# A one-token attention and gated-MLP kernel: residual rows ahead of the gate, later block jumps, wo in two loads, another syncing engine, and one wait for both stores

## The chip, the cores and the metric

One core of a Trainium2 chip. The metric is the device time of one execution in microseconds (us); medians of several executions are given. The profile's own span, from the program's first instruction to the end of its last, is about 2 us shorter than the device time. A load has "landed" when the last of the 16 DMA engines that share it has reported to its semaphore. The "tail" is what follows the attention loop, and "the granted clock" is the share of its full clock at which TensorE was allowed to run.

## The reference, cut to what matters

One decoding step for a batch of 2: layer norm, attention of 32 heads over a cache of 8192 positions, then layer norm and a gated MLP (ReLU gate). Everything is bf16.

```python
h  = x + attention(layernorm(x), k_cache, v_cache, wq, wo)   # x: (2, 1, 512)
n  = layernorm(h)
gate, up = n @ W_gate, n @ W_up                              # (512, 1376) each
h2 = h + (relu(gate) * up) @ W_down                          # W_down: (1376, 512)
```

The two caches are 134 MB each and are read once; all weights together are 12.6 MB. So about 281 MB have to cross from HBM (281.06 MB read, by the page) for a few KB of input and output rows.

## The kernel before

Each engine has a list of operations with waits. The lists of TensorE, VectorE and ScalarE are printed in three blocks (all, last, rest): an engine runs the first part, jumps to "rest", and jumps back to "last" for the end; `s.cut(engine)` marks where "last" begins. The tail of the kernel, which is all that the change touches, looks like this:

```python
WO = ((0, 0, JG), (1, 0, JG // 2), (1, JG // 2, JG))      # wo in three loads (SyncE's queue)
# ... then gate, up0, up1 (three quarters and one quarter of W_up), and W_down as wda, wdb, wdc, wdd
# ... attention rows (TensorE), transpose, ar = copy of the rows (ScalarE), mean, hd = h - mean
s.op("pe", lambda: mlp_in(0, gate_ps, 0, KC), reads=["hd", "gate"], ...)
# variance (TensorE); r2, gt = relu(gate) * r2 (VectorE)
up_mostly = s.op("pe", lambda: mlp_in(1, up_ps, 0, KC - 1), reads=["hd", "up0"], ...)
s.wait("pe", [s.last["up1"]])
s.op("pe", lambda: mlp_in(1, up_ps, KC - 1, KC), reads=["hd", "up1"], ...)
s.cut("pe")
s.op("pe", lambda: y_rows(eye_of[:, 0:B], ar, first=True), reads=["eye", "om"], writes=["y"])  # residual
# gn (VectorE)
s.wait("dve", [up_mostly])
s.cut("dve")
# actr = gt * up, actn = gn * up (VectorE); columns_of_act, columns_of_rest (TensorE)
s.wait("act", [s.last["up1"]])
s.cut("act")
s.op("act", lambda: act.activation(out=act_t[:, 0:FA], in_=act_ps, func=ACT.Copy), reads=["sm"], ...)
# add_y over wda, wdb, wdc, wdd: 8 + 8 + 4 + 2 matmuls into y; VectorE and ScalarE copy half of y each
# two stores (SyncE and ScalarE); then
s.wait("pool", ends)                                      # both stores landed
s.lists["pool"].append(((), lambda: pool.sem_clear(range(min(sems), max(sems) + 1)), None))
```

The softmax here doesn't subtract the row's maximum and nothing guards it: scores larger than these inputs give would overflow.

## Time and profile before

| | before |
|---|---|
| device time, median of 3 | 658.21 us (658.06 to 658.22) |
| span of the profile | 656.2 us |
| VectorE busy | 612.7 us (93%) |
| data moved | 281.12 MB, 428 GB/s over the span |
| last weight packet moved | 652.60 us |
| last landing of W_down | 653.08 us |
| last store landed | 655.24 us |

The page's first part, a row of busy time, share of the span and instructions for each engine, and its line for the data queue (packets, MB, share of the time of 16 DMA engines):

```profile
PE 120.3 (18%) x1212; PEld 49.8 (8%) x1212; DVE 612.7 (93%) x172; ACT 63.2 (10%) x161; POOL 6.4 (1%) x27
q1 hardware_dynamic: 6596, 281.06, 99.3%
```

Two resources are nearly full. The 99.3% is the one to read as the bound: VectorE's 93% leaves it 43 us of idle time, while the 0.7% that the data queue lacks is less than what lies before its first packet (1.97 us) and behind its last weights.

### The profile page before, as it was taken

What the parts mean: (1) busy time and instruction counts of PE and PEld (TensorE: products, weight loads), DVE (VectorE), ACT (ScalarE), POOL (GpSimd) and SP (SyncE); (2) the same over time, 40 slices, a digit from 0 to 9 for tenths busy, and PEclk for the clock granted to TensorE, in tenths of its full rate; (3) what the DMA queues carried; (4) which work ended last, traced back from release to release, by engine and by line L of the source; (5) the groups of instructions that cost most, each with busy time, mean ns of one, the idle gap of its engine ahead of it and who ended that gap; (6) DMA issues with size and microseconds to landing.
All of it is one profiled execution on the core that took longest, in us unless ns stands there. A gap on an engine that the chain in (4) does not pass through costs nothing.

```text
span 656.2 us, 3121 instructions
## 1 busy us (share of the span) xinstructions
PE 120.3 (18%) x1212; PEld 49.8 (8%) x1212; DVE 612.7 (93%) x172; ACT 63.2 (10%) x161; POOL 6.4 (1%) x27
## 2 busy tenths in 40 slices
PE   2400302103030110302003030300303030031256
PEld 1100101001010000101001010100101010010012
DVE  0699999999999999999999999999999999999973
ACT  2501001010101001010100101010010101001021
POOL 3000000000000000000000000000000000000000
PEclk9855755657565565756556575555657556565756
DMA  9999999999999999989999999989999999999997
GB/s 380 451 443 411 423 447 447 423 407 447 447 447 391 439 447 447 443 387 447 447 447 415 415 447 447 443 387 447 447 447 427 403 447 447 443 403 432 425 420 311
DMA packets 6613, 281.12 MB, mean 428 GB/s; under 512 B 744, under 2 KB 848, under 8 KB 1360
## 3 DMA queue, kind: packets, MB, share of 16 engines
q1 hardware_dynamic: 6596, 281.06, 99.3%
q8 instruction: 2, 0.03, 0.0%
q14 instruction: 3, 0.02, 0.0%
q10 hardware_dynamic: 12, 0.01, 0.0%
HBM read 281.06 MB, written 0.00 MB: 428 GB/s over the span
## 4 chain that ended last, share of the span: by engine, by line
DVE 75%; DMA 24%; issue 0%; SPq 0%; PE 0%
DVE k L386 34%; DVE k L391 33%; DMA k<-in_A_k_cache_dram 21%; DVE sc L243 4%; DMA k<-in_B_W_down_dram 3%; DVE osb L471 2%; DVE om L466 1%; SPq L547 0%; DVE ou L243 0%; SPq L559 0%; DVE rep L478 0%; PE y L641 0%; DVE sc L721 0%; SPq L294 0%; SPq L805 0%
## 5 line engine op out<-in xcount | busy, mean ns | idle before, releaser
L386 DVE TENSOR_TENSOR k<-k,qrep 128x32768 bf16<-128x32768 bf16 (+3 forms) x18 | 275.8, 15322 | 6.2 <-DMA k<-in_A_k_cache_dram 6.1
L391 DVE TENSOR_TENSOR k<-k 128x8192 bf16<-128x8192 bf16 (+4 forms) x69 | 266.9, 3868 | 2.4
L417 PE MATMUL o<-v,pm 128*32 128x512 bf16 x1024 | 93.8, 544 | 478.8 <-PEq L432 478.8
L404 ACT ACTIVATE pm<-sc 32x256 bf16<-32x256 f32 (+2 forms) x68 | 48.0, 705 | 560.1 <-DVE sc L243 559.3
L417 PEld LDWEIGHTS o<-v,pm 128*32 128x32 bf16 x1024 | 38.5, 130 | 533.5 <-issue 527.7
L243 DVE TENSOR_REDUCE sc<-k 128x256 f32<-128x2048 bf16 (+2 forms) x17 | 36.6, 2151 | 0.1
L471 DVE TENSOR_REDUCE osb<-om 128x128 f32<-128x512 f32 x16 | 16.3, 1018 | 0.6
L404 ACT ACTIVATION_READ_ACCUMULATOR pm<-sc 32x1 f32 x68 | 15.7, 231 | 0.0
L466 DVE TENSOR_TENSOR om<-o,turn_of 128x512 f32<-128x512 f32 x16 | 10.9, 682 | 3.9 <-PE o L417 3.9
L350 PE MATMUL mm<-v,om 128*64 x32 | 9.5, 432 | 6.6 <-PEq L348 6.6
L243 DVE TENSOR_REDUCE pick<-ident 128x8 f32<-128x128 bf16 x1 | 0.4, 382 | 10.7 <-ACT qrep L367 10.7
L367 ACT ACTIVATE qrep<-mm 32x512 bf16<-32x512 f32 x16 | 9.4, 587 | 6.1 <-PE mm L350 5.2
L451 PE MATMUL rep<-osb,spread 128*32 128x128 f32 x32 | 2.6, 421 | 37.1 <-DVE osb L471 37.1
L538 POOL TENSOR_TENSOR zm<-zm,zx 128x1 f32<-128x1 f32 x1 | 0.2, 192 | 625.9 <-PE o L417 625.9
L320 DVE COPY xc<-st 128x8 f32<-128x8 f32 x1 | 0.2, 167 | 6.5 <-PE st L315 6.5
L350 PEld LDWEIGHTS mm<-v,om 128*64 128x64 bf16 x32 | 3.9, 121 | 11.8 <-issue 11.0
L607 DVE STREAM_TRANSPOSE osb<-mm 128x512 f32<-128x512 f32 x1 | 0.7, 716 | 3.8 <-PE mm L593 3.8
L593 PE MATMUL mm<-k 128*2 128x512 bf16 x32 | 3.8, 621 | 0.3 <-DMA k<-in_A_wo_dram 0.3
L451 PEld LDWEIGHTS rep<-osb,spread 128*32 128x32 f32 x32 | 0.8, 140 | 37.5 <-DVE osb L471 37.5
L446 PE MATMUL sm<-zm,same 128*128 128x16 f32 x8 | 1.8, 297 | 0.4 <-PEq L432 0.4
L721 DVE CAST sc<-y 2x256 bf16<-2x256 f32 x1 | 0.4, 413 | 1.5 <-PE y L641 1.5
L240 POOL MEMSET pm<- 128x2048 bf16 x1 | 1.8, 1805 | 0.1
(81 smaller groups left out, 34.9 us busy)
## 6 DMA issues: line engine op xcount, KB each, us to landing
v<-in_A_v_cache_dram SPq DMA_DIRECT2D x4, 4096.0 KB, 20.3
k<-in_A_k_cache_dram SPq DMA_DIRECT2D x2, 4096.0 KB, 26.3
v<-in_A_wq_dram SPq DMA_DIRECT2D x1, 4096.0 KB, 12.4
k<-in_A_wo_dram SPq DMA_DIRECT2D x1, 2048.0 KB, 20.2
k<-in_A_wo_dram SPq DMA_DIRECT2D x2, 1024.0 KB, 23.2
k<-in_B_W_gate_dram SPq DMA_DIRECT2D x1, 1376.0 KB, 13.2
k<-in_B_W_up_dram SPq DMA_DIRECT2D x1, 1032.0 KB, 15.3
k<-in_B_W_down_dram SPq DMA_DIRECT2D x2, 512.0 KB, 17.0
```

The source lines that it names most:

```text
L240: s.op("pool", lambda: pool.memset(pm, 0.0), writes=["pm"])
L243: s.op("dve", lambda: dve.tensor_reduce(out=out_, in_=in_, axis=axis, op=ALU.add), reads=reads, writes=writes)
L350: last = pe.matmul(out=mm_ps[t][0:B * Q], lhsT=xnb[:, c].rearrange("p b q -> p (b q)"), rhs=wq_r[:, c, :, bass.ds(r * 2 + t, 1), :], start ...
L367: fn = lambda src=src, dst=dst: act.activation(out=dst, in_=src, func=ACT.Copy)
L386: s.op("dve", lambda: dve.tensor_tensor(out=kp, in0=kp, in1=_view(qrep[:, b, i, :], 0, [[0, hi - lo], [1, Dh]]), op=ALU.mult), reads=keys ...
L391: s.op("dve", lambda half=half, width=width: dve.tensor_tensor(out=kp[:, :, 0:half], in0=kp[:, :, 0:half], in1=kp[:, :, half:width], op=AL ...
L404: last = act.activation(out=p_of[ps, lo // TG:hi // TG, :, h], in_=sc2[n % 2][ps, lo:hi].rearrange("p (g t) -> p g t", t=TG), func=ACT.Exp ...
L417: last = pe.matmul(out=o_ps[g:g + W2], lhsT=pm[:, t // TG, :], rhs=vt[:, t:t + TG, :].rearrange("p t d -> p (t d)"), start=(t < P // Q * T ...
L451: last = pe.matmul(out=rep_ps[u * Q:(u + 1) * Q, :], lhsT=spread.rearrange("k h m -> k (h m)"), rhs=osb[:, u, :], start=True, stop=True, s ...
L466: s.op("dve", lambda: dve.tensor_tensor(out=om.rearrange("p (t d) -> p t d", d=Dh), in0=o_ps.rearrange("p (t d) -> p t d", d=Dh), in1=_vie ...
L471: s.op("dve", lambda: dve.tensor_reduce(out=osb[:, n % NS, :], in_=om.rearrange("p (t d) -> p d t", d=Dh), axis=AXIS.X, op=ALU.add), reads ...
L593: last = pe.matmul(out=ar_ps[g:g + B], lhsT=oc[:, k, :], rhs=wo_sb[:, k, :], start=False, stop=(k + P // Q >= NK), skip_group_check=True)
```

## The change

Its intent is to shorten the tail: residual matmuls off the way between up and the columns of act, block jumps to where the engine has nothing urgent to do, fewer loads, and a semaphore clear that no longer waits for the stores. Cut to its core:

```diff
-    ctx.enter_context(tc.tile_critical(no_gpsimd_drain=True))
+    ctx.enter_context(tc.tile_critical(
+        sync_engine=mybir.EngineType.Activation, no_gpsimd_drain=True))
-    WO = ((0, 0, JG), (1, 0, JG // 2), (1, JG // 2, JG))
+    WO = ((0, 0, JG), (1, 0, JG))
+    s.op("pe", lambda: y_rows(eye_of[:, 0:B], ar, first=True), reads=["eye", "om"], writes=["y"])
     s.op("pe", lambda: mlp_in(0, gate_ps, 0, KC), reads=["hd", "gate"], writes=["gate_o"])
 # ... up ...
     s.cut("pe")
-    s.op("pe", lambda: y_rows(eye_of[:, 0:B], ar, first=True), reads=["eye", "om"], writes=["y"])
-    s.wait("dve", [up_mostly])
-    s.cut("dve")
 # ... actr, actn on VectorE ...
+    s.wait("dve", [s.last["act"]])
+    s.cut("dve")
 # ... columns on TensorE ...
-    s.wait("act", [s.last["up1"]])
-    s.cut("act")
     s.op("act", lambda: act.activation(out=act_t[:, 0:FA], in_=act_ps, func=ACT.Copy), ...)
+    s.wait("act", [s.last["act_t"]])
+    s.cut("act")
 # ... stores: both now add to one semaphore y_out; each engine adds 1 to "gone" once its store is issued ...
-    s.wait("pool", ends)
-    s.lists["pool"].append(((), lambda: pool.sem_clear(...), None))
+    s.wait("pool", [("gone", 2)])
+    s.lists["pool"].append(((), clear, None))          # every semaphore but y_out
+    s.lists["pool"].append(
+        ((), lambda: pool.wait_ge(s.sem("y_out"), 32).then_inc(s.sem("y_out"), -32), None))
```

More of the change, by code (lines that the diff above doesn't have):

```diff
@@ L219, with clear @@
     sm_ps = psum("sm", (P, 512))
-    s = Streams(nc, ("pe", "dve", "act", "pool", "sp"))
+    s = Streams(nc, ("y_out", "pe", "dve", "act", "pool", "sp"))
+    def clear():
+        sems = [h.num for k, h in s.sems.items() if k != "y_out"]
+        pool.sem_clear(range(min(sems), max(sems) + 1))
     for name in ("v_in", "v_two", "p_in", "p_two", "o_in", "half", "q0", "q1", "z_in", "z_out"):
@@ L666 @@
         reads=["gate_o", "r2"], writes=["osb0", "osb1", "osb2", "osb3"])
-    up_mostly = s.op("pe", lambda: mlp_in(1, up_ps, 0, KC - 1), reads=["hd", "up0"],
-                     writes=["mm1"])
+    s.op("pe", lambda: mlp_in(1, up_ps, 0, KC - 1), reads=["hd", "up0"], writes=["mm1"])
     s.wait("pe", [s.last["up1"]])
@@ L723 @@
          writes=["y1"])
-    ends = []
     for c, rows, eng, e in ((0, y0, "sp", sync), (1, y1, "act", act)):
-        ends.append(s.dma(eng, f"dy{c}", lambda c=c, rows=rows, e=e: e.dma_start(
+        s.op(eng, lambda c=c, rows=rows, e=e: e.dma_start(
             out=out.rearrange("b s d -> (b s) d")[:, c * D // 2:(c + 1) * D // 2],
-            in_=y_row[rows]), reads=[f"y{c}"]))
-    sems = [h.num for h in s.sems.values()]
-    s.wait("pool", ends)
-    s.lists["pool"].append(((), lambda: pool.sem_clear(range(min(sems), max(sems) + 1)), None))
+            in_=y_row[rows]), reads=[f"y{c}"], gives=("y_out", 16))
+        s.lists[eng].append(((), lambda e=e: e.sem_inc(s.sem("gone"), 1), None))
+    s.wait("pool", [("gone", 2)])
+    s.lists["pool"].append(((), clear, None))
+    s.lists["pool"].append(
+        ((), lambda: pool.wait_ge(s.sem("y_out"), 32).then_inc(s.sem("y_out"), -32), None))
     engines = (("sp", sync), ("pool", pool), ("act", act), ("pe", pe), ("dve", dve))
     inner = nc.cur_bb
+    for name in [w for ops in s.lists.values() for waits, _, gives in ops
+                 for w in [k for k, _ in waits] + ([gives[0]] if gives else [])]:
+        s.sem(name)
     for name, engine in engines:
```

## The prediction

> **What bounds the kernel now.** I read the page first (busy shares, DMA slices), then the chain that ended last, the stretches of 2 us over the end, the timeline of the last 25 us, and last the trace's records of semaphores and landings. VectorE looks like the bound at 93% busy, but the DMA row says otherwise:
>
> ```profile
> DMA  9999999999999999989999999989999999999997
> DMA packets 6613, 281.12 MB, mean 428 GB/s; under 512 B 744, under 2 KB 848, under 8 KB 1360
> ```
>
> No slice before the last is under eight tenths, and in the DMA records no instant between the first data packet at 1.97 us and the last weight packet at 652.60 us is without a packet in flight. The kernel is one uninterrupted stream of 281 MB, and whatever happens beside it (VectorE's work on the keys included) is hidden unless it starves the queue. The change touches none of the loop's loads, so only three places can move the time: when the stream starts, how long it is, and what follows it. The chain shows what follows:
>
> ```profile
> 635.21 17.67 DMA k<-in_B_W_down_dram
> 652.88 0.14 issue
> 653.02 0.51 PE y L641 x6
> 653.53 0.02 issue
> 653.55 0.41 DVE sc L721
> ```
>
> The last weights land (the third part of W_down at 652.88, the 96 KB fourth at 653.08 in the landing records), TensorE does the six matmuls that need them, and VectorE and ScalarE each copy half a row and store it. Before that, the timeline shows a compute chain running nearly level with the stream:
>
> ```profile
> 642.89 1.02 PE L593 MATMUL mm<-k 128*2 128x512 bf16 x8 [0.30 <-DMA k<-in_A_wo_dram]
> 643.97 0.72 DVE L607 STREAM_TRANSPOSE osb<-mm 128x512 f32<-128x512 f32 x1 [3.81 <-PE mm L593]
> 645.69 0.29 DVE L627 TENSOR_TENSOR sc<-xc,st 128x128 bf16<-128x128 f32 x1 [0.42 <-PE st L623]
> 646.29 1.40 PE L651 MATMUL gate<-k,sc 128*32 128x344 bf16 x16 [0.71 <-DVE sq L634]
> 648.68 1.41 PE L651 MATMUL mm<-k,sc 128*32 128x344 bf16 x16 [0.48 <-DMA k<-in_B_W_up_dram]
> 649.24 0.53 DVE L673 TENSOR_TENSOR qrep<-osb,head_blk 128x352 f32<-128x352 f32 x1
> 650.23 1.28 ACT L707 ACT_TABLE_LOAD   x1 [4.91 <-DMA k<-in_B_W_up_dram]
> 650.39 1.02 PE L641 MATMUL y<-om,eye_of 128*2 128x256 f32 x4 [0.30 <-issue]
> 650.69 0.42 DVE L679 TENSOR_TENSOR qrep<-osb,mm 128x256 bf16<-128x256 f32 x1 [0.92 <-PE mm L651]
> 651.59 0.18 ACT L707 ACTIVATE k<-sm 128x16 bf16<-128x16 f32 x1
> 651.83 1.04 PE L641 MATMUL y<-k 128*2 128x256 bf16 x16
> 653.02 0.49 PE L641 MATMUL y<-k 128*2 128x256 bf16 x6 [0.15 <-DMA k<-in_B_W_down_dram]
> 653.55 0.38 ACT L722 ACTIVATE sc<-y 2x256 bf16<-2x256 f32 x1 [1.77 <-PE y L641]
> ```
>
> See three waits for the stream, at 642.89, 648.68 and 653.02: there the chain had slack of 0.3, 0.48 and 0.15 us. (The gate group is put down to VectorE, but its weights land only at 646.15 in the records, later than its operand, 645.98.) See also the 0.92 us before L679, though up ended at 650.09: VectorE was jumping to another block. Its wait ended at 649.83 and its first instruction there ran at 650.69, so a jump is 0.86 us; ScalarE's was 649.57 to 650.23, 0.66 us.
>
> [...] TensorE's last branch took 1.84 us. [...] the stores were issued at 653.96 and 653.99 and landed at 655.07 and 655.24, about 1.1 and 1.25 us.
>
> **The change, part by part.**
>
> *wo in two loads.* 256 packets of 8 KB become 128 of 16 KB. In the records an 8 KB packet takes 313.4 ns and a 16 KB one 614.9 ns, so each pair saves 11.9 ns; 8 pairs on each of 16 engines save 0.095 us, and one semaphore write of 9.5 ns goes too. The stream ends 0.10 us sooner, and every landing after it. The price is on TensorE: eight matmuls that ran from 641.52, before the last piece landed, must now wait for it. Four matmuls advance in 0.43 us, so eight cost 0.85 us. Less 0.10 us, the transpose moves from 643.97 to 644.72, and hd's end from 645.98 to 646.73.
>
> *Residual rows ahead of the gate.* They take about 0.76 us of TensorE's issue (two passes, 0.38 us apart, from the records at 650.39 and 650.77). Their operand (ScalarE's copy, 644.72 + 0.60, moved by 0.75) is there at 646.08; TensorE is free after the mean's matmul at about 646.2. So they run to about 646.95, and the gate starts at 646.9 instead of 646.29: +0.6. It ends 0.6 later, then the variance matmul until about 648.84. Up's weights land at 648.54, so up is late by only about 0.15 (648.84 against 648.68): the old 0.48 us of slack swallows most. Up ends at about 650.24.
>
> *VectorE jumps behind the norm.* r2, gt and gn follow the variance, +0.63, so gn ends about 650.38. L679 then needs no jump and starts about 650.35, against 650.69: -0.34. TensorE has no residual rows in the way. ScalarE's copy of the columns starts at about 651.24 (was 651.59), the 16 matmuls at 651.48. They now meet the stream: the second part of W_down landed at 652.14 before, 652.04 now. VectorE's jump, from 650.8 to 651.66, lies beside this; its columns are needed only at 652.88.
>
> *What the gain is worth.* The final six matmuls wait for the landings at 652.78 and 652.97 and end about 653.41 instead of 653.51. Of 0.34 us gained in the chain nothing beyond the stream's 0.10 arrives.
>
> *ScalarE's table load.* The block that ScalarE jumps to begins with it. The jump now comes after the copy (ends 651.42): 0.66 of jump and 1.28 of load give 653.39. The row's second half is ready at 653.45. It fits, with 0.06 us to spare.
>
> *ScalarE as the section's syncing engine.* At the start it swaps who does the no-op at 0.72 and who waits for it; SyncE's first load (0.95) might be 0.03 us earlier. I count 0.03. At the end it swaps who collects.
>
> *One wait for both stores, with the clear before it.*
>
> ```profile
> L731 POOLq EVENT_SEMAPHORE_RANGE_CLEAR  x1: 117/117/117, 655.3 to 655.3; - x1
> ```
>
> This clear waited for the last store, so its 0.117 us lay on the path to the final barrier. Now it lies beside the store's 1.2 us; the decrement in its place costs about 0.02. So -0.10. TensorE reports to the barrier only at 655.08 because of its 1.84 us branch; with 0.10 us off that it is 654.98, just ahead of the landing at 655.14, so it does not take over.
>
> *Sum:* -0.10 (stream) - 0.10 (clear) - 0.03 (start) = -0.23 us of 658.21: 657.98, say 658.0.
>
> **Rivals.** *The compute chain becomes the bound.* If the 0.85 us of wo and the 0.76 us of residual rows came through in full, the end would be about 1 us later: 659.2. For it: both are certainly put in front of the norm. Against: up's 0.48 us of waiting and the 0.86 us jump lie behind them. *The table load ends last.* With 0.06 us of margin a small slip in the chain puts ScalarE's half row last; if ScalarE's copy stays at 651.59, its half row starts at 653.7 and the time is about 658.3. For it: the margin is thinner than my steps are certain. Against: only the overrun counts, and ScalarE's store landed 0.17 us before SyncE's. [...] *The removed jump pays in full*: if the weights landed earlier than I think, -0.34 more: 657.6; against it stand the landing records.
>
> **Range and chances.** All terms are tenths of a us; the three runs of before span 0.16 us and another chip or run may shift by a few tenths. Range 657.4 to 658.7. 2% would be 13 us, more than all that follows the attention loop's last product; I give 0.99 to "same".
>
> **What would show it.** Right: last packet of W_down about 0.1 us earlier relative to the first; the transpose about 0.75 us later, up almost in place, L679's counterpart about 0.3 us earlier and without a jump ahead of it; the second group of eight y matmuls waiting for W_down; the table load after the copy of columns, ending close to 653.4; the semaphore clear ahead of the stores' landing. Wrong: a chain whose last wait is the table load or ScalarE's copy rather than W_down; the gate or up more than 0.5 us late; a first load that starts at another time than 0.95 us.

## The result, and the profile after

The changed kernel took 658.02 us (median of 6, 657.80 to 658.39) against 658.22 us of before (median of 6): ratio 0.9997, 95% interval 0.9984 to 1.001. On another occasion it had 657.68 us against 658.33 us, ratio 0.999 (0.9976 to 1.0003). A ratio is the mean time of one kernel's fast runs over that of the other's of the same rounds, so it is not quite the ratio of the medians. Both intervals hold 1: the time is the same within 2%, and a saving of a few tenths is suggested twice but not resolved by timing.

The timeline of the changed kernel's tail (start, length, engine, line, operation, and in brackets the idle time before it with what ended it):

```profile
642.54 1.87 PE L599 MATMUL mm<-k 128*2 128x512 bf16 x16 [2.23 <-DMA k<-in_A_wo_dram]
644.47 0.72 DVE L613 STREAM_TRANSPOSE osb<-mm 128x512 f32<-128x512 f32 x1 [4.83 <-PE mm L599]
646.01 1.02 PE L647 MATMUL y<-om,eye_of 128*2 128x256 f32 x4
646.53 1.69 PE L657 MATMUL gate<-k,sc 128*32 128x344 bf16 x16
648.67 1.41 PE L657 MATMUL mm<-k,sc 128*32 128x344 bf16 x16
650.23 0.41 DVE L682 TENSOR_TENSOR qrep<-osb,mm 128x256 bf16<-128x256 f32 x1
650.95 0.18 ACT L710 ACTIVATE k<-sm 128x16 bf16<-128x16 f32 x1 [5.13 <-PE sm L697]
651.28 1.04 PE L647 MATMUL y<-k 128*2 128x256 bf16 x16
651.82 1.28 ACT L727 ACT_TABLE_LOAD   x1 [0.69 <-ACT k L710]
652.64 0.70 PE L647 MATMUL y<-k 128*2 128x256 bf16 x6 [0.32 <-DMA k<-in_B_W_down_dram]
653.39 0.38 ACT L727 ACTIVATE sc<-y 2x256 bf16<-2x256 f32 x1 [0.29 <-PE y L647]
```

Line by line against before: the transpose is 0.50 us later although wo landed 0.45 us earlier (642.40 against 642.85), so the merge costs 0.95 us there; up starts where it started (648.67 against 648.68); the product of gate and up is 0.46 us earlier and has no idle time ahead of it; the copy of the columns is 0.64 us earlier; and then the last six matmuls wait for W_down, as they did. The chain that ended last says the same:

```profile
637.90 15.12 DMA k<-in_B_W_down_dram
653.03 0.04 issue
653.07 0.29 PE y L647 x2
653.37 0.02 issue
653.39 0.41 DVE sc L726
```

It ends with the fourth load of W_down, landed at 653.03 (653.08 before). The copies start at 653.39 instead of 653.55. At the end of the program the clear now stands ahead of the stores' landing at 655.09, and is longer (287 ns instead of 117), as it covers more semaphores (with fourteen more, in the kernel with wo in sixteen loads, it took 355 ns):

```profile
L226 POOLq EVENT_SEMAPHORE_RANGE_CLEAR  x1: 287/287/287, 654.2 to 654.2; - x1
```

From the last store's landing to the end of the span it is 0.90 us, where it was 0.98.

### The profile page after: what moved, and what is told of

The parts are those of the page before. It is cut to its first block, busy times and chain, and to the rows that moved or that the text cites. A ratio compares the mean times of both kernels' runs of the same rounds, so it can differ in the third digit from the quotient of the medians.

```text
span 656.0 us, 3124 instructions
## 1 busy us (share of the span) xinstructions
PE 121.9 (19%) x1212; PEld 50.5 (8%) x1212; DVE 612.5 (93%) x172; ACT 63.3 (10%) x161; POOL 6.5 (1%) x27
## 5 line engine op out<-in xcount | busy, mean ns | idle before, releaser
L423 PE MATMUL o<-v,pm 128*32 128x512 bf16 x1024 | 95.8, 553 | 477.0 <-PEq L438 477.0
```

What stands on the lines that cost most here:

```text
L423: last = pe.matmul(out=o_ps[g:g + W2], lhsT=pm[:, t // TG, :], rhs=vt[:, t:t + TG, :].rearrange("p t d -> p (t d)"), start=(t < P // Q * T ...
```

## The experiments

Theory: the end follows the last landing of W_down, and the compute chain before it is hidden. Rivals: the parts of the change cancel inside a chain that binds; or ScalarE's moved table load binds. Twelve kernels ran, all correct. Kernels are compared only within the same rounds. The table has the moments read from each trace (us), which the sections below use; "end" is the span, "rest" the span less the last landing of the weights.

| kernel | transpose | product | 16 y matmuls end | last landing | end | rest | device time, median |
|---|---|---|---|---|---|---|---|
| before | 643.97 | 650.69 | 652.87 | 653.08 | 656.22 | 3.14 | 658.2 |
| changed | 644.47 | 650.23 | 652.32 | 653.03 | 655.98 | 2.95 | 658.02 |
| changed, again | 644.62 | 650.38 | 652.49 | 653.42 | 656.38 | 2.96 | 657.68 |
| before, wo in two | 644.89 | 650.82 | 652.92 | 653.54 | 656.57 | 3.03 | 658.55 |
| changed, wo in three | 643.85 | 650.08 | 652.64 | 653.09 | 656.43 | 3.34 | 658.44 |
| changed, wo in sixteen | 644.17 | 650.80 | 653.40 | 653.86 | 657.38 | 3.52 | 659.30 |
| changed, old ending | 644.60 | 650.36 | 652.46 | 653.07 | 656.10 | 3.03 | 657.83 |
| changed, VectorE's jump early | 644.53 | 650.73 | 652.84 | 653.17 | 656.15 | 2.98 | 658.01 |
| changed, residual rows late | 644.42 | 649.88 | 652.28 | 653.36 | 656.31 | 2.95 | 658.17 |
| changed, ScalarE's jump early | 644.72 | 650.47 | 652.65 | 652.95 | 656.01 | 3.06 | 658.00 |
| changed, SyncE enters | 644.53 | 650.33 | 652.43 | 652.91 | 656.02 | 3.11 | 658.19 |

The product moves over 0.94 us and the transpose over more than 1 us from row to row, and the end does not follow them: apart from wo in sixteen loads, it is the last landing plus 2.95 to 3.34 us.

### The changed kernel again

No edit.

> The changed kernel again, to see how much the end of the stream moves from one execution to another: if the 0.4 us by which up's weights landed earlier in its first trace belong to the change, they land again near 649.1; if they are scatter of one slow DMA engine, they land anywhere between 649.1 and 649.5. Time 657.8 to 658.4.

Measured: 657.68 us (657.63 to 658.24). Up's last quarter landed at 649.29, between the 649.11 of the first trace and the 649.55 of before. In the trace of before one of the 16 DMA engines reports 0.32 to 0.36 us behind the fifteenth for every load of the tail but the last two; in the two traces of the changed kernel that lag is 0.04 to 0.07. Of the other traces with the loads in this order, three have 0.11 to 0.34 (wo in two on the kernel before; wo in three; ScalarE's jump early), the rest 0.01 to 0.13. So most of the 0.4 us is scatter between executions, and only the rest can be the change's. This last landing came at 653.42, later than in either trace before it, with the device time of that execution at 658.24: the same kernel's end moves by 0.4 us with it.

### The merge of wo by itself

```diff
 # on the kernel before
-    WO = ((0, 0, JG), (1, 0, JG // 2), (1, JG // 2, JG))
+    WO = ((0, 0, JG), (1, 0, JG))
```

> The kernel before with only wo in two loads. Stream theory: the transpose about 0.5 us later (near 644.5), VectorE's product gt*up about 0.5 us later (near 651.2, because gn is later and the jump follows it), the 16 y matmuls near 652.35 and ended near 653.4, past the last landing of W_down (653.03 to 653.08), so here the compute chain takes over by 0.3 us: time of before plus 0.1 to 0.4 us, 658.3 to 658.6. Rival (the wo merge is free because up waits for its weights anyway): product at 650.7 as before and no change of time.

Measured: 658.55 us (657.98 to 658.65), ratio 1.0002 (0.9988 to 1.0016): no difference resolved. Its chain that ended last:

```profile
635.34 17.72 DMA k<-in_B_W_down_dram
653.06 0.14 issue
653.19 0.38 PE y L641 x4
```

The expectation that the compute chain takes over failed. The transpose moved by 0.92 us, but up by only 0.13 (648.81) and the product by 0.13 (650.82). The jump of VectorE is released by up's first twelve matmuls and runs beside the product of gate and head mask, which ended at 650.44 and left only 0.37 us of idle time ahead of the product of gate and up, so the later norm did not push it. The longer end of this trace comes from its last landing at 653.54. The delay of the merge is thus absorbed by up's wait for its weights even without the rest of the change, as the rival in this expectation said.

### wo in three loads again

```diff
 # on the changed kernel
-    WO = ((0, 0, JG), (1, 0, JG))
+    WO = ((0, 0, JG), (1, 0, JG // 2), (1, JG // 2, JG))
```

> The changed kernel with wo in three loads again. Stream theory: transpose about 0.5 us earlier (near 644.0), gate bound by its landing, product gt*up near 650.0, but the end again set by the last landing of W_down: time within 0.15 us of the changed kernel (658.0), the stream longer by 0.1 us of packet time (128 pairs of 8 KB for 128 of 16 KB). Rival (the merge's delay is what eats the gain of the other parts): 0.3 to 0.5 us faster than the changed kernel, 657.5 to 657.7.

Measured: 658.44 us (657.86 to 658.91), ratio to before 1.0004 (0.999 to 1.0018): not faster. The transpose came at 643.85, the earliest of all, and the product at 650.08, the earliest but one, and yet the rest behind the last landing was the longest of those with few loads. The stretches of 1 us show why (after the busy times come the granted TensorE clock, the DMA share and GB/s):

```profile
652.00:653.00 1.00, 0.60 (x8) 0.29 (x9) 0.00 (x0) 0.95 (x1) 0.00 (x0) 1.00 0.26 66
653.00:654.00 1.00, 0.80 (x6) 0.23 (x6) 0.16 (x1) 0.16 (x1) 0.00 (x0) 0.52 0.00 0
```

The granted clock fell from 1.00 to 0.52 just as the last six matmuls began at 653.00; they took 0.80 us. In the first trace of the changed kernel the last two took 0.29 us behind the landing at a clock of 1.00. In both traces this stretch of full clock lasts 3.4 us (649.6 to 653.0 here, 650.7 to 654.2 there); the other ones in the trace of before and in the first of the changed kernel last 3.4 or 6.8 us, and one in each 10.2 us. Whether an earlier chain caused the earlier grant here, or chance, one trace cannot say. In the same group of runs the kernel with wo in two loads and the old ending took 657.83 us (657.73 to 657.99), 0.6 us less than this one, which is more than the 0.1 us of packets; so the merge may be worth more than the stream theory gives it, through the clock or otherwise. That is not settled here.

### wo in sixteen loads

```diff
 # on the changed kernel
-    WO = ((0, 0, JG), (1, 0, JG))
+    WO = tuple((k, lo, lo + 2) for k in range(2) for lo in range(0, JG, 2))
```

> The changed kernel with wo in sixteen loads of 2 KB rows: a larger dose of the packet cost. At 86 ns for a packet of 2 KB against 615 ns for one of 16 KB, 16 times 86 against 2 times 615 is 0.15 us more for a partition, times 8 partitions on an engine is 1.2 us more of stream, all of it at the end: stream theory 658.0 + 1.2 = 659.2 us and every landing of W_down 1.2 us later. Rival (the end is set by the compute chain, or packet cost overlaps in the engines): 658.0 to 658.3.

Measured: 659.30 us (659.04 to 659.56), ratio 1.0016 (1.0002 to 1.0029): the only small difference that timing resolves. Its chain that ended last (the third load of W_down, at 653.51, was at 652.51 in the first trace of the changed kernel):

```profile
637.27 16.25 DMA k<-in_B_W_down_dram
653.51 0.14 issue
653.65 0.77 PE y L647 x6
```

The summed packet time per DMA engine rose by 1.42 us (652.20 against 650.78), and the last landing came 0.83 us later than in the first trace of the changed kernel (0.44 us later than in the second), at 653.86. Against the first trace, the remaining 0.57 us of the span lie behind the landing: the last six matmuls ran partly at a lower clock (0.87 granted over 653 to 654 us instead of 1.00; they ended 0.55 us behind the landing instead of 0.32), and SyncE reported to the last barrier only at 656.44, behind the landing of the stores at 656.14; why so late is not shown. Packet cost at the end of the stream is paid in time: the direction is as expected and the packet sum a little above it (1.42 us for 1.2), and of the 1.2 to 1.3 us of time 0.83 are the stream's in that comparison. The change's own step from 8 to 16 KB (two packets of 313.4 ns for one of 614.9) is the same effect at about a tenth of the dose (0.05 to 0.17 us of packet time).

### VectorE's jump early

```diff
 # on the changed kernel
+    s.wait("dve", [up_mostly])
+    s.cut("dve")
     s.op("dve", lambda: dve.tensor_tensor(out=actr, ...
-    s.wait("dve", [s.last["act"]])
-    s.cut("dve")
```

> The changed kernel with VectorE's jump back ahead of gt*up. Stream theory: the product starts 0.7 to 1.0 us later (near 651.1), the 16 y matmuls near 652.2 and ended near 653.2, just past the last landing of W_down (653.03); ScalarE's table load after its jump ends near 654.0 and its half row comes last: time 658.0 + 0.4 to 0.7. Rival (chain hidden with room to spare): 658.0.

Measured: 658.01 us (657.82 to 658.34), ratio 0.9995 (0.9982 to 1.0009): no loss. The product came 0.35 to 0.5 us later than in the two traces of the changed kernel, less than the 0.7 to 1.0 expected, as the jump again ran partly beside VectorE's own work (0.36 us idle ahead of the product, for a jump of 0.86). Here the rival of the table load shows:

```profile
652.32 1.28 ACT L728 ACT_TABLE_LOAD   x1 [0.69 <-ACT k L711]
653.53 0.41 DVE L727 CAST sc<-y 2x256 bf16<-2x256 f32 x1 [1.46 <-PE y L647]
653.62 0.37 ACT L728 ACTIVATE sc<-y 2x256 bf16<-2x256 f32 x1
```

ScalarE's half row waits for its own table load, 0.09 us behind VectorE's, and its store is the last one issued (654.02 against 653.97). With ScalarE's jump behind its copy the table load can bind, and is kept off the end by the earlier product. In time nothing was lost by it.

### Residual rows late

```diff
 # on the changed kernel: y_rows(eye_of, ar, first=True) from ahead of the gate to behind up's last quarter
```

> The changed kernel with the residual rows back behind up. They then stand ahead of the columns of act: those at 651.4 instead of 650.7, ScalarE's copy at 651.7, its table load 652.55 to 653.85. Table-load rival: the half row of ScalarE starts at 653.85 instead of 653.39, time 658.3 to 658.5. If the table load is not what counts, TensorE's six last matmuls end near 653.5 and the time is 658.0 to 658.15.

Measured: 658.17 us (658.06 to 658.81), ratio 1.0 (0.9986 to 1.0013). The expected chain did not come about. At the clock granted then (1.00 instead of 0.50) the rows took 0.60 us (649.91 to 650.51), not 1.02, and without them ahead of it the gate began 0.05 us earlier and took 1.40 us instead of 1.69: columns at 650.44, table load ended at 652.84, a margin of 0.88 us. In this setting moving the rows forward gains nothing that can be seen.

### ScalarE's jump early

```diff
 # on the changed kernel
+    s.wait("act", [s.last["up1"]])
+    s.cut("act")
     s.op("act", lambda: act.activation(out=act_t[:, 0:FA], ...
-    s.wait("act", [s.last["act_t"]])
-    s.cut("act")
```

> The changed kernel with ScalarE's jump back ahead of its copy of the columns: the table load then runs from 649.8 to 651.1 and the copy starts at 651.1 to 651.4 instead of 650.95, the 16 matmuls up to 0.4 us later, ended by 652.8, still before the last landing of W_down at 653.03: no change of time (657.9 to 658.2), and 0.3 us more room for ScalarE's half row. Rival (ScalarE's copy is on the path): plus 0.3 us.

Measured: 658.00 us (657.91 to 658.63), ratio 0.9999 (0.9985 to 1.0012). As expected: the table load ran from 650.06 to 651.34 and held the copy to 651.35, the 16 matmuls ended at 652.65, still ahead of the third and fourth landing (652.75, 652.95).

### The old ending

```diff
 # on the changed kernel: the stores, the wait and the clear as in the kernel before
```

> The changed kernel with the old ending: GpSimd waits for both stores, then clears. Step as predicted: 0.1 us of clear back on the path between the last store's landing and the final barrier, so 0.1 us (up to 0.2) from the landing to the end of the span more than in the changed kernel, where it is 0.90 us (655.08 to 655.98). Rival (TensorE's late arrival at the barrier hides it): no difference. Time 658.0 to 658.3, not to be told apart by timing; the trace decides.

Measured: 657.83 us (657.73 to 657.99), ratio 0.9994 (0.998 to 1.0007). From the last store's landing (655.14) to the end 0.96 us; in the changed kernel, in its repetition and in four of its variants with the new ending (wo in three, and each of the three moves undone) it is 0.89 to 0.90. So the clear gives 0.07 us, not 0.10: from the start of the clear to the next instruction it was 0.17 us before, and from the start of the wait with the decrement that stands in its place it is 0.10. No timing could show this.

### SyncE as the syncing engine

```diff
 # on the changed kernel
-    ctx.enter_context(tc.tile_critical(
-        sync_engine=mybir.EngineType.Activation, no_gpsimd_drain=True))
+    ctx.enter_context(tc.tile_critical(no_gpsimd_drain=True))
```

> The changed kernel with SyncE as the section's syncing engine again: first load issued at 0.95 instead of 0.92 us, first packet at 1.97 instead of 1.94; from the last store's landing to the end the same 0.90 us. Time 657.8 to 658.4, not to be told apart. Rival (ScalarE as syncing engine costs or saves at the end): 0.05 us or more from the landing to the end.

Measured: 658.19 us (657.88 to 658.70), ratio 0.9999 (0.9985 to 1.0012). The first load was issued at 0.95 instead of 0.92 us, the first packet moved at 1.96 instead of 1.94, and from the last landing to the end it was 0.92 instead of 0.90 us. The swap is worth about 0.02 us at either end.

### W_down ahead of gate and up, on both kernels

```diff
 # on the kernel before, and on the changed kernel
+    load_down("wda", ...); load_down("wdb", ...); load_down("wdc", ...); load_down("wdd", ...)
     for key, g, w, c0, c1 in (("gate", ...), ("up0", ...), ("up1", ...)):   # moved behind them
```

> The kernel before with the four loads of W_down issued ahead of gate and up: the same bytes, but the stream now ends with up's last quarter, so that the compute chain behind up is no longer covered by it. Stream theory: the last landing stays near 653.05, now that of up, and everything behind up is exposed: VectorE's product near 654.0 (after its jump), columns of act near 654.65 (behind the residual rows), ScalarE's copy near 655.0, last y matmul near 656.7, about 3.6 us from the last landing to the last y matmul where it is 0.4 now; time about 661.4. Rival (the end is set by the compute chain, whatever the order of the loads): within 0.5 us of 658.2.

> The changed kernel with W_down first in the same way. What the change does for the chain should now be seen: product near 653.6, columns near 654.05, ScalarE's copy near 654.3, last y matmul near 656.05: 0.65 us sooner than in the kernel before with W_down first. But ScalarE's table load, 0.67 us of jump and 1.28 us behind its copy, ends near 656.45 and holds its half row: of the 0.65 us about 0.25 to 0.3 reach the store, plus 0.07 at the ending; time about 661.0, 0.2 to 0.6 us under the other. Rival (the change does nothing for the chain): equal. Rival (the table load does not bind): 0.7 us under.

Measured: 661.32 us (661.06 to 661.37) and 661.01 us (660.62 to 661.70), ratios to the kernel before 1.0044 (1.0031 to 1.0058) and 1.0041 (1.0028 to 1.0055). Both are 3 us slower with the same bytes, which settles that the present order of the loads covers the compute chain. The change's gain in the chain shows up to the copy of the columns: 1.38 us behind up's last landing (653.09) instead of 1.97 (652.84). Then it is lost in the traced executions. The kernel before with W_down first, from its timeline and from its stretches of 1 us (the third number from the right is the granted TensorE clock):

```profile
655.11 1.36 PE L642 MATMUL y<-k 128*2 128x256 bf16 x22
```

```profile
655.00:656.00 1.00, 1.00 (x21) 0.81 (x23) 0.17 (x1) 0.00 (x0) 0.00 (x0) 1.00 0.00 0
```

The same two views of the changed kernel with W_down first, with its table load:

```profile
654.82 1.94 PE L648 MATMUL y<-k 128*2 128x256 bf16 x22
655.34 1.28 ACT L728 ACT_TABLE_LOAD   x1 [0.69 <-ACT k L711]
```

```profile
655.00:656.00 1.00, 1.00 (x12) 0.62 (x10) 0.17 (x1) 0.66 (x1) 0.00 (x0) 0.50 0.07 16
```

The 22 matmuls took 1.94 us at a clock of 0.50 instead of 1.36 at 1.00, so they ended at 656.76, 3.67 us behind up's landing against 3.63. The table load, ended at 656.63, was 0.17 us short of binding: the expectation that it would take half of the gain failed, the clock took all of it in this execution. The traced execution (661.25 us) was the second slowest of its five, though. The two medians differ by 0.31 us, inside the expected 0.2 to 0.6, but the two ranges overlap, so how much of the gain usually arrives stays open. Whether the moved rows, which had kept TensorE busy at 653.68 to 654.28 in the kernel before, have to do with the grant is not shown by one trace of each.

### An attempt at a faster version: the values' load before the last in one piece

```diff
 # on the changed kernel
-        if n + 1 < NLOOP - 1:
+        if n + 1 < NLOOP:
             load_v(n + 1)
 # and the credit for the unsplit loads: 16 * (NLOOP - 1) becomes 16 * NLOOP
```

> An attempt at a better version on the stream theory: the values' load before the last goes whole (64 KB rows) instead of in two halves. From the records 64 KB take 2422 ns and 32 KB 1227 ns, so 32 ns are saved for a partition and 8 times that on an engine, 0.26 us of stream: summed packet time 650.5 instead of 650.76 us, time 657.7 if the queue does not starve while VectorE and TensorE finish the tile before. Rival (the load now waits for the whole of the tile before it, and the queue runs dry): over 658.5.

Measured: 664.05 us (663.79 to 664.60), ratio 1.0087 (1.0074 to 1.0101): 6 us slower. The stretch of 610 to 620 us in this kernel, and then the same stretch in the kernel before (the last number is GB/s, the one before it the DMA share):

```profile
610.00:620.00 10.00, 6.04 (x64) 2.47 (x64) 9.72 (x5) 0.00 (x0) 0.00 (x0) 0.58 0.30 102
```

```profile
610.00:620.00 10.00, 3.61 (x32) 1.27 (x32) 9.90 (x5) 0.00 (x0) 0.00 (x0) 0.66 1.05 452
```

The unsplit load has to wait for all of the tile before it, and the queue ran dry: in the DMA records no packet of it is in flight from 612.61 to 618.17 us, 5.56 us, against the 6 us that were lost. The saving that was hoped for did not show either: the summed packet time was 651.19 us per engine, not 650.5. It is a failed version, and the plainest evidence for the bound: a hole in the stream is paid in full, while half a microsecond in the chain is not paid at all. No experiment gave a version faster than the changed kernel by more than the scatter.

## Why the prediction was right, point by point

The predicted 658.0 us, the range and "same" held (658.02). The mechanism held too: the stream binds, and the change's own work disappears behind it. By its steps:

- **Stream 0.10 us shorter.** About right where it can be summed: packet time per engine (semaphore writes left out) was 650.93 us in the kernel before and 650.92 in the changed kernel with wo in three loads, 650.78 and 650.76 in the two traces of the changed kernel; the merge alone, on the kernel before, had 650.88. So the saving was 0.05 to 0.17 us. The last weight packet ended at 652.10 and 652.38 instead of 652.60. But no saving arrived reliably at the end: the last landing was 653.03 and 653.42 against 653.08. In eight of the ten traces with the loads in their present order (wo in sixteen left out) the sixteenth engine was 0.12 us or more behind the fifteenth at the last load, up to 0.59 us, whatever the kernel; a 16 KB instruction packet moved at that time in every one of them (started between 651.7 and 652.1 us) and took 1.2 to 1.6 us, where a weight packet of that size took 0.61. That it holds up an engine's last weights is a guess that was not tested: in seven of the ten traces it ended only after the last landing, and the records used here do not tell which engine carried it. What starts that packet stays open.
- **wo costs 0.85 us at the transpose.** Measured 0.95 from landing to transpose (1.12 before, 2.07 after).
- **Residual rows push the gate by 0.6 us.** Too much: the rows fitted almost wholly into TensorE's wait for hd, and the gate began with hd, at 646.53 instead of the predicted 646.9; in the changed kernel it took 0.29 us longer for it. Up began at 648.67 (predicted 648.84).
- **Product 0.34 us sooner.** Measured 0.46 and 0.31 in the two traces. With VectorE's jump put back, the product was only 0.35 to 0.5 us later than without it, though the jump is 0.86 us long, as it ran partly beside VectorE's own instructions.
- **None of it arrives.** Right: the last matmuls waited for W_down in both traces of the changed kernel, and the end went with the last landing in every row of the table.
- **Table load 0.06 us from binding.** Its own terms (651.42 + 0.66 + 1.28) give 653.36, not 653.39, so a margin of 0.09. Measured 0.29 us in the first trace and 0.53 in the second; with VectorE's jump put back it did bind, by 0.09 us.
- **Clear 0.10 us, start 0.03 us.** Measured about 0.07 and 0.02 to 0.03.
- **The signs it named.** One sign of being right did not come: in the first trace the second group of eight y matmuls did not wait for W_down, as the second part landed at 651.67, not at 652.04, and the sixteen ran through from 651.28 to 652.32. And one sign of being wrong did come, a first load at another time than 0.95 us: it was at 0.92, which is only the 0.03 us that the prediction itself counts.

The rival of the compute chain failed in the experiment that gave it the best chance, the merge of wo alone (up moved by 0.13 us). TensorE's report to the barrier did not take over: it came at 654.94, before the landing at 655.09. The predicted sum of -0.23 us agrees with the -0.20 us of the medians, but the execution-to-execution scatter of the last landing alone is 0.4 us, so the agreement of this number is partly luck; what is shown is the bound and the size of the parts in the traces.

## What to carry to other kernels

Before shortening a tail, look for the landing that it ends with: if every variant of the compute chain waits there, the gain is slack and nothing more. What moved the time or the end here was how the bytes were packed (1.42 us of packet time for wo in sixteen loads), an uninterrupted queue (6 us), what the stream ended with (3 us with up last), and what comes after the last landing (0.07 us of clear). Slack gained in such a place still has a use, as it pays for what would otherwise bind (here a table load of 1.28 us behind a jump). And where the effects are tenths of a microsecond, read moments in several traces rather than medians, as the granted clock (22 matmuls took 1.36 us at 1.00 and 1.94 at 0.50) and one late DMA engine (up to 0.59 us behind the fifteenth) move a single end by as much.

## What else the traces measured

- A jump to a block took 0.66 us on ScalarE and 0.86 us on VectorE from the end of its wait to the first instruction, in the traces of before and of the changed kernel; the branch ahead of the program's end took 1.84 and 1.74 us on TensorE there. What fills this time is not shown. A jump ran beside an instruction already given to the engine: with VectorE's jump early, two branches ran between 649.97 and 650.33, beside the product of 649.84 to 650.37, and of the 0.86 us only 0.35 to 0.5 were paid.
- The 16 KB instruction packet at the end of the last loads took 1.61 us in the trace of before and 1.49 in the first of the changed kernel, against 0.61 us for a weight packet of that size. A second one, after all weights had landed, took 1.37 and 1.32 us, so those loads are not all of it.
- The table load took 1.28 us. With VectorE's jump early the copy started 0.01 us behind the end of the load (653.61 to 653.62).
- The 16 engines of one DMA finished at different times: in the trace of before one engine was 0.32 to 0.36 us behind the fifteenth at load after load, and in the changed kernel's two traces at most 0.07 us, the last two loads left out.
